# One decode step of attention and MLP: 512 rows of wo over eight DMA engines in place of 320 over five

## The chip, the cores and the metric

The kernel runs on one core of one Trainium2 chip. The metric is the device time of one execution, in microseconds (us); a kernel is timed several times, and its median is given. A profile is of one execution more: its span runs from the first instruction to the last, and its own time is some two microseconds longer than that span. Engines go by these names: PE does the matmuls (PEld its weight loads), DVE and ACT work on vectors, POOL on little here, and SP issues the DMAs. Sixteen DMA engines move the data of the core. A DMA is cut into packets, which are spread over some or all of the sixteen; it has landed when the last packet of its last engine has.

## The reference, cut to what matters

One token is computed, with 32 heads of 128 and the last 4096 keys and values of a cache of 32768 each. Beside attention stands a small MLP on the same normalized x, and its SiLU gates the attention's output:

```
W = min(4096, max(256, Sk // 4))                    # 4096
q = (x @ wq).reshape(B, Sq, Hq, Dh)                 # x: 1 x 512, wq: 512 x 4096
scores = einsum("bhqd,bhkd->bhqk", q, k[last W]) * (Dh ** -0.5)
p = softmax(scores)
o = einsum("bhqk,bhkd->bhqd", p, v[last W])
s = o.reshape(B, Sq, Hq * Dh) @ wo                  # wo: 4096 x 512
...
xn = layernorm(A_x)
return A_x + s * silu(B(xn, w1, w2, w3, w4))
```

All tensors are bf16. The keys and values that are read are 32 MB each, wq and wo 4 MB each, the MLP's weights that are read some 3.3 MB. Row r of wo belongs to head r // 128.

## The kernel before, in words

Heads are taken in groups of four (`G = 4`), so there are eight groups, 0 to 7. For each group one DMA of 4 MB loads the keys (K0 to K7) and one the values (V0 to V7), 32 KB for each of 128 partitions; K0 comes in two pieces and V7 in three (`cuts = (0, 64, 112, CP)`, line 509: 64, 48 and 16 of the 128 columns). The main loop (line 514) has steps s = 0 to 9. Step s computes the scores of group s, the softmax of group s - 1 and the products with the values of group s - 2 (`LAG = 2`). The scores are shared: DVE multiplies and sums some of the columns (`k_vector`, lines 304 to 311), and PE transposes the others, ACT copies them out, and PE multiplies them with q (`k_turn`, `k_scores`). `v_part` (line 417) multiplies probabilities with values, one small matmul a column, and `v_out` (line 440) scales the result to o.

All loads go out from SP, in the order of the program (`load`, line 78). The buffers set when: three for keys, two for values. V7's first load, for instance, has to wait until PE is done with V5.

The product with wo is taken in blocks of heads as they come ready (`blocks`, line 385): heads 0 to 15 in `y_wide`, heads 16 to 23 in `y_block(1)`, and the last eight heads, 24 to 31, in pieces, all summed in one PSUM tile `y_ps`:

- **The few** (`wo_few`): the first FEW = 8 * 8 * NE rows of head 24 on; with NE = 5 these are 320 rows, that is heads 24 and 25 and half of head 26. `load_few` (line 398) loads them with two DMAs. Each has 4 * NE partitions with 8 rows each, which lie together in memory, so that a packet is 8 KB; its outermost dimension in memory is NE, and it runs on NE engines. The tile has 64 partitions, 32 for each DMA; what the loads do not fill is zeroed by POOL (line 522). `ox_few` (line 478) brings o into the same order with a small matmul, whose selection tile `few` is built at lines 264 to 269, and `y_block(few_block)` multiplies in 8 x 4 matmuls.
- **The rows** (`wo_rows`): the rest, head by head, 1 KB for each partition. `load_rows` (line 408) loads them: first, ahead of V7, the second half of head 26 (64 rows, on partitions 64 to 127; the first half of that tile is zeroed by POOL, line 524) and head 27 (128 rows); then, behind V7's three pieces, heads 28 and 29 in one DMA and heads 30 and 31 in one each. `y_head` (line 505) multiplies one head in 4 matmuls.

Group 6 is heads 24 to 27, group 7 heads 28 to 31. The few and the rows of heads 26 and 27 thus need o of group 6 alone, the last four heads need o of group 7. The last step (lines 597 to 606) runs on PE in this order: V7's first 64 columns, the few, heads 26 and 27 (lines 600 and 601), V7's other two pieces, and after `v_out` heads 28 to 31. DVE then multiplies with the gate and adds x, and SP writes the output (lines 608 to 612). The order of PE, DVE and ACT in the loop is that of the program (`tc.manual_schedule`).

The queue of SP, with what concerns the change, is at its end: ... V5, wo of heads 16 to 23, the two loads of the few, V6, the two loads of heads 26 and 27, V7 in three pieces, heads 28 and 29, head 30, head 31, output.

Of the kernel before, what the change touches and what calls it, by code (L numbers as in the profile page):

```python
# [8 lines left out]
P = 128  # L9
# [9 lines left out]
G = 4  # L19
LAG = 2  # L20
K_BUFS = 3
NE = 5
V_BUFS = 2
EARLY = 2
LATE = 7
# [4 lines left out]
def kernel(  # L30
# [14 lines left out]
    nc = tc.nc  # L45
# [3 lines left out]
    _, H, Sk, Dh = A_k_cache.shape  # L49
# [28 lines left out]
    def load(dst, src):  # L78
        return tc.keep_in_program_order(nc.sync.dma_start(out=dst, in_=src))
# [17 lines left out]
    def load_kv(pool, cache, g, cuts=(0, CP)):  # L97
        t = pool.tile([P, CP, Dh], BF16, tag="kv", name="kv")
        src = cache[0, G * g:G * g + G, W0:, :].rearrange("a (b c) d -> b a (c d)", b=PB)
        dst = t[:].rearrange("p c d -> p (c d)")  # L100
        for c0, c1 in zip(cuts, cuts[1:]):
            load(dst[:, c0 * Dh:c1 * Dh], src[:, :, c0 * Dh:c1 * Dh])
        return t
# [43 lines left out]
    def rows_add(ps, col, w, last):  # L147
        k = col.shape[0]
        for j in range(KC):
            nc.tensor.matmul(ps[32 * j:32 * j + 1, :], lhsT=col, rhs=w[0:k, j * P:(j + 1) * P],  # L150
                             start=False, stop=last, skip_group_check=True)
# [114 lines left out]
    for c in range(2):  # L266
        nc.vector.tensor_copy(
            out=few[:, c, 0:4 * NE].rearrange("p (a b) -> p a b", b=4),
            in_=ident_bf[:, 4 * NE * c:4 * NE * (c + 1)].rearrange("p (b a) -> p a b", b=4))

# [27 lines left out]
    def k_open(g):  # L298
        st[g] = {
            "sT": ps_s.tile([P, CP - 64, G], FP32, tag="sT", name="sT"),  # L300
            "S": sm_pool.tile([P, CP], FP32, tag="S", name="S"),
        }

    def k_vector(g, kn, part):
        m = nd(g) // 4
        rows = slice(m * part, m * part + m)
        prod = prod_pool.tile([P, 20, Dh], BF16, tag="prod", name="prod")
        nc.vector.tensor_tensor(out=prod[:, 0:m, :], in0=kn[:, rows, :],  # L308
                                in1=q_bc[:, g:g + 1, :].to_broadcast([P, m, Dh]), op=ALU.mult)
        nc.vector.tensor_reduce(out=st[g]["S"][:, rows], in_=prod[:, 0:m, :], axis=AX.X, op=ALU.add)  # L310
# [3 lines left out]
    def batches(g):  # L314
        n, m = nd(g), CP - nd(g)
        k = -(-m // 8)
        edges = [n + m * i // k for i in range(k + 1)]
        return list(zip(edges, edges[1:]))

    def k_turn(g, kn, b):  # L320
        c0, c1 = batches(g)[b]
        pt = ps_tr.tile([P, 8, P], BF16, tag="pt", name="pt")
        for c in range(c0, c1):
            nc.tensor.transpose(pt[:, c - c0, :], kn[:, c, :], ident_bf[:])  # L324
        kts[b] = kt_pool.tile([P, 8, P], BF16, tag="kt", name="kt")
        nc.scalar.copy(out=kts[b][:, 0:c1 - c0, :], in_=pt[:, 0:c1 - c0, :])  # L326

    def k_scores(g, b):
        kt = kts.pop(b)
        c0, c1 = batches(g)[b]  # L330
        for c in range(c0, c1):
            nc.tensor.matmul(st[g]["sT"][:, c - nd(g), :], lhsT=kt[:, c - c0, :],  # L332
                             rhs=qT_bf[:, G * g:G * g + G], start=True, stop=True)
# [39 lines left out]
    def sm_den(g):  # L373
        s = st[g]
        s["den"] = ps_misc.tile([P, G], FP32, tag="misc", name="den_ps")
        nc.tensor.matmul(s["den"][:], lhsT=ones_f[:], rhs=s["sum"][:], start=True, stop=True)  # L376

    def sm_rden(g):
        s = st[g]
        s["rden"] = sm_pool.tile([P, G], FP32, tag="rden", name="rden")  # L380
        nc.vector.reciprocal(out=s["rden"][:], in_=s["den"][:])  # L381
# [5 lines left out]
    few_h = blocks[few_block][0]  # L387
    FEW = 8 * 8 * NE
    h_part = few_h + FEW // P

    r_part = FEW % P
    o_blk, wo_blk, ox_blk = {}, {}, {}

    def load_wo(i):
        h0, n = blocks[i]
        load(wo_blk[i], A_wo[h0 * P:(h0 + n) * P, :].rearrange("(p t) n -> p t n", p=P))

    def load_few():
        t = wo_blk[few_block]
        for c in range(2):  # L400
            r0 = few_h * P + c * FEW // 2
            load(t[32 * c:32 * c + 4 * NE],
                 A_wo[r0:r0 + FEW // 2, :].rearrange("(b a t) n -> a b (t n)", b=4, a=NE))

    def wo_row(h):
        return wo_rows[:, h - h_part, :]

    def load_rows(h, n):
        if h == h_part:
            load(wo_rows[r_part:P, 0, :], A_wo[h * P + r_part:(h + 1) * P, :])  # L410
            h, n = h + 1, n - 1
        load(wo_rows[:, h - h_part:h - h_part + n, :],
             A_wo[h * P:(h + n) * P, :].rearrange("(h p) n -> p h n", p=P))

# [86 lines left out]
    def y_block(i):  # L501
        for t in range(8):
            rows_add(y_ps, ox_blk[i][:, t:t + 1], wo_blk[i][:, t, :], False)

    def y_head(h):
        rows_add(y_ps, o_blk[few_block][:, h - few_h:h - few_h + 1], wo_row(h), h == H - 1)
# [7 lines left out]
    for s in range(NG + LAG):  # L514
        h = s - LAG
        last = h == NG - 1
        kn = load_kv(k_pool, A_k_cache, s, (0, 64, CP) if s == 0 else (0, CP)) if s < NG else None
        if s == LAG:
            wts_guard.__exit__(None, None, None)
            v_pool = ctx.enter_context(tc.tile_pool(name="v", bufs=V_BUFS))  # L520
            wo_blk[few_block] = v_pool.tile([64, 8, D], BF16, tag="wo_few", bufs=1, name="wo_few")
            nc.gpsimd.memset(wo_blk[few_block][:], 0.0)
            wo_rows = v_pool.tile([P, H - h_part, D], BF16, tag="wo_rows", bufs=1, name="wo_rows")
            nc.gpsimd.memset(wo_rows[0:r_part, 0, :], 0.0)
        if last:
            load_rows(h_part, 2)
            v = load_kv(v_pool, A_v_cache, h, cuts)
            for r, n in ((H - G, 2), (H - 2, 1), (H - 1, 1)):
                load_rows(r, n)
        elif h >= 0:  # L530
            v = load_kv(v_pool, A_v_cache, h)
        if h == 3:
            wo_24 = k_pool.tile([P, 32, D], BF16, tag="kv", name="wo_24")
            wo_blk[0], wo_blk[1] = wo_24[:, 0:16, :], wo_24[:, 16:24, :]
            load_wo(0)
        if h == 5:
            load_wo(1)
            load_few()

        if s < NG:  # L540
            nb = len(batches(s))

            def keys(b0, b1):
                for b in range(b0, b1):
                    k_turn(s, kn, b)
                    if b > 0:
                        k_scores(s, b - 1)

            k_open(s)
            k_vector(s, kn, 0)  # L550
            keys(0, 2)
            if s > 1:
                sm_den(s - 2)
                sm_rden(s - 2)
            if h - 1 in MOVED:
                v_add(h - 1)
                v_out(h - 1)
            keys(2, 4)
            k_vector(s, kn, 1)
            if s > 0:  # L560
                sm_turn(s - 1)
            if s == 6:
                ox_spread(0)
            keys(4, nb)
            k_scores(s, nb - 1)
            sm_own(s)
            if s > 0:
                sm_exp(s - 1)
            k_vector(s, kn, 2)
            if s == 6:  # L570
                ox_pick(0)
            k_vector(s, kn, 3)
            if h >= 0:
                v_part(h, v)
            sm_max(s)
            if s == 6:
                y_wide(0, 0, 16)
            if h >= 0 and h not in MOVED:
                v_out(h)
        elif s == NG:  # L580

            sm_den(NG - 2)
            sm_rden(NG - 2)
            sm_turn(NG - 1)
            ox_spread(1)
            sm_exp(NG - 1)
            ox_pick(1)
            y_block(1)
            rows_add(y_ps, one_f, y_row, False)
            v_part(h, v)  # L590
            v_out(h)
            ox_spread(few_block)
            sm_den(NG - 1)
            sm_rden(NG - 1)
            ox_pick(few_block)
            ox_few(few_block)
        else:
            v_part(h, v, 0, cuts[1])
            y_block(few_block)
            for r in range(h_part, H - G):  # L600
                y_head(r)
            for c0, c1 in zip(cuts[1:], cuts[2:]):
                v_part(h, v, c0, c1)
            v_out(h)
            for r in range(H - G, H):
                y_head(r)
# [36 lines left out]
```

## Time and profile before

| what | value |
|---|---|
| median of 4 runs | 195.07 us (194.64 to 196.91) |
| profiled execution, its own time | 195.71 us |
| its span | 193.9 us |
| mean granted TensorE clock | 0.682 |
| read from HBM | 78.84 MB, 407 GB/s over the span |
| load queue of SP (q1) | 4554 packets, 96.0% of 16 engines' span |
| wo_few loads | 2 of 160 KB, issued from 131.16 us on |
| wo_rows loads ahead of V7 | 64 KB and 128 KB, issued from 151.04 us on |
| V7's three pieces | 2048, 1536 and 512 KB, issued from 172.21 us on |

How to read it: times within the profile count from the span's start. The profiled execution took 195.71 us, 0.64 us above the median of the runs. A DMA's share is the mean over the 16 engines, so that a share of 13/16 can mean that three of them have nothing to do. A share can come out a little over 1, since packets on one engine overlap by some nanoseconds and count where they start. Packets of the DMA queues named "instruction" carry program text to the engines.

### The profile page before, as it was taken

To read this page: it belongs to the slowest core of one execution; us is meant where nothing else is said; L and a number is where in the kernel's file an instruction comes from. 1 tells how busy PE (TensorE), PEld (TensorE's weight loads), DVE (VectorE), ACT (ScalarE), POOL (GpSimd) and SP (SyncE) were. 2 spreads that over 40 slices of the span, in tenths; PEclk is the share of its full clock that TensorE was granted. 3 is DMA by queue.
4 is the path that set the end of the run, shared out by engine and by line. 5 is a ranking of instruction groups with operands and counts; after the bars stand their busy time and mean duration, and the time that the engine had idled before them with its cause. 6 is when DMAs were issued, how large, how long until landed. Compare 5 with 4: busy or idle time off the path is not lost.

```text
span 193.9 us, 4769 instructions
## 1 busy us (share of the span) xinstructions
PE 134.5 (69%) x2123; PEld 102.5 (53%) x2123; DVE 143.8 (74%) x162; ACT 87.2 (45%) x195; POOL 6.4 (3%) x14
## 2 busy tenths in 40 slices
PE   0559761978746579697998978730788878854892
PEld 0453451867535433386985347730768246743771
DVE  1550109998999999999999999990899999951201
ACT  2003001889896360467577155720485059813000
POOL 2110008000000000000000000000000000000000
PEclk9999965586955558965555896855555599655555
DMA  6999999999999999999999999999999999999980
GB/s 213 419 450 365 379 429 478 426 433 422 433 422 433 433 428 429 433 433 433 436 429 439 422 439 389 470 422 422 439 433 431 426 429 397 465 411 369 418 332 14
DMA packets 4725, 79.13 MB, mean 408 GB/s; under 512 B 666, under 2 KB 1466, under 8 KB 1722
## 3 DMA queue, kind: packets, MB, share of 16 engines
q1 hardware_dynamic: 4554, 78.84, 96.0%
q8 instruction: 16, 0.26, 0.5%
q10 hardware_dynamic: 152, 0.00, 0.0%
q14 instruction: 3, 0.02, 0.0%
HBM read 78.84 MB, written 0.00 MB: 407 GB/s over the span
## 4 chain that ended last, share of the span: by engine, by line
DMA 38%; DVE 33%; PE 16%; ACT 9%; issue 2%; SPq 0%; ACTq 0%
DMA kv<-in_A_k_cache_dram 29%; DVE S L310 19%; DVE prod L308 11%; DMA kv<-in_A_v_cache_dram 8%; ACT kt L326 7%; PE oT L430 5%; PE pt L324 4%; PE yr_ps L496 3%; PE sT L332 2%; DMA x_bf<-in_A_x_dram 2%; ACT o L453 1%; PE den_ps L376 1%; PE oT L437 1%; DVE S L346 1%; PE mb_ps L363 1%
## 5 line engine op out<-in xcount | busy, mean ns | idle before, releaser
L310 DVE TENSOR_REDUCE S<-prod 128x20 f32<-128x2560 bf16 (+2 forms) x32 | 82.2, 2570 | 1.1
L326 ACT COPY kt<-pt 128x1024 bf16<-128x1024 bf16 (+1 forms) x56 | 54.5, 1006 | 23.9 <-PE pt L324 23.2
L324 PE MATMUL pt<-ident_bf,kv 128*128 128x128 bf16 x444 | 46.7, 275 | 10.9 <-DMA kv<-in_A_k_cache_dram 10.9
L308 DVE TENSOR_TENSOR prod<-kv,q_bc 128x2560 bf16<-128x2560 bf16 (+2 forms) x32 | 43.5, 1359 | 8.5 <-DMA kv<-in_A_k_cache_dram 5.6
L324 PEld LDWEIGHTS <-kv 128*128 128x128 bf16 x444 | 37.7, 126 | 12.9 <-DMA kv<-in_A_k_cache_dram 11.2
L332 PE MATMUL sT<-qT_bf,kt 128*128 128x4 bf16 x444 | 20.7, 168 | 15.9 <-ACT kt L326 15.3
L332 PEld LDWEIGHTS <-kt 128*128 128x128 bf16 x444 | 17.1, 104 | 23.8 <-ACT kt L326 23.7
L430 PE MATMUL oT<-pT,kv 128*128 128x4 bf16 x768 | 22.0, 166 | 5.4 <-issue 3.6
L430 PEld LDWEIGHTS <-kv 128*128 128x128 bf16 x768 | 21.3, 104 | 7.4 <-issue 4.1
L422 PE MATMUL ov<-kv,pT 128*16 128x512 bf16 x64 | 17.5, 441 | 0.0
L370 ACT ACTIVATE pT<-S,mb 128x128 bf16<-128x128 f32 x32 | 13.9, 569 | 0.3
L422 PEld LDWEIGHTS <-pT 128*16 128x16 bf16 x64 | 6.3, 101 | 10.2 <-issue 4.6
L453 ACT ACTIVATE o<-oT,rden 128x1 bf16<-128x1 f32 x24 | 4.3, 261 | 11.8 <-PE oT L430 7.6
L449 DVE TENSOR_TENSOR o<-oT,rden 128x4 bf16<-128x4 f32 x2 | 0.3, 162 | 12.3 <-PE oT L430 12.3
L341 ACT ACTIVATE own<-sT,par 128x48 f32<-128x48 f32 (+2 forms) x32 | 7.6, 360 | 3.7 <-PE sT L332 3.7
L370 ACT ACTIVATION_READ_ACCUMULATOR pT<-S,mb 128x1 f32 x32 | 8.2, 255 | 0.0
L425 ACT COPY ov_sb<-ov 16x512 f32<-16x512 f32 x2 | 1.1, 575 | 13.2 <-PE ov L422 13.2
L231 DVE COPY hr<-hr_ps 1x512 f32<-1x512 f32 x1 | 0.7, 678 | 8.1 <-PE hr_ps L228 8.1
L496 PE MATMUL yr_ps<-wo,ox 128*1 128x512 bf16 x16 | 5.9, 545 | 0.9 <-DVE ox L474 0.9
L220 ACT ACTIVATE a_bf<-a_ps 128x10 bf16<-128x10 f32 x1 | 0.2, 180 | 11.8 <-PE a_ps L217 11.8
L363 PE MATMUL mb_ps<-md,par_t 5*128 5x4 f32 x16 | 4.2, 330 | 1.7 <-DVE md L358 1.0
L354 PE MATMUL mt_ps<-ident_f,m 128*1 128x128 f32 x8 | 2.8, 346 | 3.6 <-DVE rden L381 3.6
(117 smaller groups left out, 90.5 us busy)
## 6 DMA issues: line engine op xcount, KB each, us to landing
kv<-in_A_k_cache_dram SPq DMA_DIRECT2D x7, 4096.0 KB, 30.2
kv<-in_A_v_cache_dram SPq DMA_DIRECT2D x7, 4096.0 KB, 34.2
wq_sb<-in_A_wq_dram SPq DMA_DIRECT2D x1, 4096.0 KB, 19.5
kv<-in_A_k_cache_dram SPq DMA_DIRECT2D x2, 2048.0 KB, 24.9
wo<-in_A_wo_dram SPq DMA_DIRECT2D x1, 2048.0 KB
kv<-in_A_v_cache_dram SPq DMA_DIRECT2D x1, 2048.0 KB, 11.8
kv<-in_A_v_cache_dram SPq DMA_DIRECT2D x1, 1536.0 KB, 14.8
w_sb<-in_B_w_dram SPq DMA_DIRECT2D x1, 1376.0 KB
```

What stands on the lines that cost most here:

```text
L308: nc.vector.tensor_tensor(out=prod[:, 0:m, :], in0=kn[:, rows, :], in1=q_bc[:, g:g + 1, :].to_broadcast([P, m, Dh]), op=ALU.mult)
L310: nc.vector.tensor_reduce(out=st[g]["S"][:, rows], in_=prod[:, 0:m, :], axis=AX.X, op=ALU.add)
L324: nc.tensor.transpose(pt[:, c - c0, :], kn[:, c, :], ident_bf[:])
L326: nc.scalar.copy(out=kts[b][:, 0:c1 - c0, :], in_=pt[:, 0:c1 - c0, :])
L332: nc.tensor.matmul(st[g]["sT"][:, c - nd(g), :], lhsT=kt[:, c - c0, :], rhs=qT_bf[:, G * g:G * g + G], start=True, stop=True)
L341: nc.scalar.mul(s["own"][:, 0:m, a], s["sT"][:, 0:m, a], par[:, a:a + 1])
L363: nc.tensor.matmul(mb_ps[:], lhsT=par_t[:].rearrange("k b a -> k (b a)"), rhs=md[:], start=True, stop=True)
L370: nc.scalar.activation(out=s["pT"][:, :, a], in_=s["S"][:], func=ACT.Exp, scale=scale, bias=mb[:, a:a + 1], accum_out=s["sum"][:, a:a + 1])
L422: nc.tensor.matmul(s["ov"][:], lhsT=s["pT"][:, c:c + 4, :].rearrange("p i a -> p (i a)"), rhs=v[:, c:c + 4, :], start=(c == 0), stop=(c == ...
L430: nc.tensor.matmul(s["oT"][:], lhsT=v[:, c, :], rhs=s["pT"][:, c, :], start=(c == 0), stop=(c == CP - 1))
L453: nc.scalar.mul(o_blk[b][:, c + k:c + k + 1], st[g]["oT"][:, k:k + 1], st[g]["rden"][:, k:k + 1])
L496: nc.tensor.matmul(yr[i][:], lhsT=ox_blk[i][:, t:t + 1], rhs=wo_blk[i][:, t, :], start=(t == 0), stop=(t == n - 1))
```

## The change

NE goes from 5 to 8. The few then are 8 * 8 * 8 = 512 rows, which are heads 24 to 27 in full: two DMAs of 32 partitions each, 256 KB each, with an outermost dimension of 8. The 64 partitions of the tile are then all filled. No rows of heads 26 and 27 are left for `wo_rows`: its tile has four heads in place of six, the two loads ahead of V7 are gone, the memset for half a head too, and `y_head` runs for heads 28 to 31 alone. The bytes that are loaded are the same in all. The diff:

```
-NE = 5
+NE = 8
...
     FEW = 8 * 8 * NE
     h_part = few_h + FEW // P
-
-    r_part = FEW % P
+    assert FEW % P == 0 and h_part == H - G
...
     def load_rows(h, n):
-        if h == h_part:
-            load(wo_rows[r_part:P, 0, :], A_wo[h * P + r_part:(h + 1) * P, :])
-            h, n = h + 1, n - 1
         load(wo_rows[:, h - h_part:h - h_part + n, :],
              A_wo[h * P:(h + n) * P, :].rearrange("(h p) n -> p h n", p=P))
...
             wo_rows = v_pool.tile([P, H - h_part, D], BF16, tag="wo_rows", bufs=1, name="wo_rows")
-            nc.gpsimd.memset(wo_rows[0:r_part, 0, :], 0.0)
         if last:
-            load_rows(h_part, 2)
             v = load_kv(v_pool, A_v_cache, h, cuts)
...
             v_part(h, v, 0, cuts[1])
             y_block(few_block)
-            for r in range(h_part, H - G):
-                y_head(r)
             for c0, c1 in zip(cuts[1:], cuts[2:]):
```

More of the change, by code (lines that the diff above doesn't have):

```diff
@@ L21 @@
 K_BUFS = 3
-NE = 5
+NE = 8
 V_BUFS = 2
@@ L389 @@
     h_part = few_h + FEW // P
-    r_part = FEW % P
+    assert FEW % P == 0 and h_part == H - G
     o_blk, wo_blk, ox_blk = {}, {}, {}
@@ L408, in load_rows @@
     def load_rows(h, n):
-        if h == h_part:
-            load(wo_rows[r_part:P, 0, :], A_wo[h * P + r_part:(h + 1) * P, :])
-            h, n = h + 1, n - 1
         load(wo_rows[:, h - h_part:h - h_part + n, :],
@@ L523 @@
             wo_rows = v_pool.tile([P, H - h_part, D], BF16, tag="wo_rows", bufs=1, name="wo_rows")
-            nc.gpsimd.memset(wo_rows[0:r_part, 0, :], 0.0)
         if last:
-            load_rows(h_part, 2)
             v = load_kv(v_pool, A_v_cache, h, cuts)
@@ L599 @@
             y_block(few_block)
-            for r in range(h_part, H - G):
-                y_head(r)
             for c0, c1 in zip(cuts[1:], cuts[2:]):
```

## The prediction, made before the changed kernel ran

> **What bounds the kernel now.** I read the page first: the busy table, the DMA row of the slices, the table of queues, and the chain. No engine is full, but the 16 DMA engines are.
>
> ```profile
> span 193.9 us, 4769 instructions
> PE 134.5 (69%) x2123; PEld 102.5 (53%) x2123; DVE 143.8 (74%) x162; ACT 87.2 (45%) x195; POOL 6.4 (3%) x14
> DMA  6999999999999999999999999999999999999980
> ...
> q1 hardware_dynamic: 4554, 78.84, 96.0%
> q8 instruction: 16, 0.26, 0.5%
> ```
>
> The load queue (q1) keeps the engines 96.0% busy from start to end: what counts is how many bytes each engine has to move, and which engine ends last. A second traffic shares them: 16 fetches of program text, 16 KB each. Their 0.5% is 0.005 x 16 x 193.9 / 16 = 0.97 us for one.
>
> Then the chain of waits in its order of time, for the end alone:
>
> ```profile
> 172.82 14.83 DMA kv<-in_A_v_cache_dram
> 187.65 0.05 issue
> 187.70 1.88 PE oT L430 x64
> 189.58 0.02 issue
> 189.61 0.17 DVE o L449
> 189.78 0.04 issue
> 189.82 0.69 PE y_ps L150 x14
> ```
>
> The end hangs on the second piece of the last values (48 columns of V7), which lands at 187.65. After it come 64 small matmuls, the scaling of o, and the products with wo's last four rows of heads.
>
> Then the timeline of the same stretch, for PE's own work ahead of that landing:
>
> ```profile
> 184.08 1.87 PE L430 MATMUL oT<-pT,kv 128*128 128x4 bf16 x64
> ...
> 186.53 0.80 PE L150 MATMUL y_ps<-wo_few,of 64*1 64x128 bf16 x23 [0.19 <-issue]
> 187.26 0.10 PEld L150 LDWEIGHTS <-o 128*1 128x1 bf16 x8 [0.22 <-issue]
> 187.26 0.38 PE L150 MATMUL y_ps<-wo_rows,o 128*1 128x128 bf16 x8
> 187.70 1.79 PEld L430 LDWEIGHTS <-kv 128*128 128x128 bf16 x64 [0.33 <-DMA kv<-in_A_v_cache_dram]
> ```
>
> PE ends its products for heads 26 and 27 at 187.64, 0.01 us before the landing. So two things end there together, and a gain needs both.
>
> Last, the quarter-microsecond windows at the end (PE busy, clock, DMA share, GB/s):
>
> ```profile
> 185.75:186.00 0.25, 0.25 (x16) 0.50 1.11 451
> 186.00:186.25 0.25, 0.25 (x9) 0.50 0.82 336
> 186.25:186.50 0.25, 0.10 (x2) 0.50 0.81 336
> ...
> 188.50:188.75 0.25, 0.25 (x16) 0.50 0.65 225
> 189.00:189.25 0.25, 0.25 (x16) 0.50 0.53 184
> 189.50:189.75 0.25, 0.07 (x3) 0.50 0.10 33
> ```
>
> This is a staircase: the engines do not end together. From 186.0 the share is 0.81 to 0.82, which is 13 of 16: three engines have nothing left 3.5 us before the last one stops. The trace's packet records, which no view prints, say the same when a packet is put on the engine whose last packet ended where it begins: three engines end at 186.1, 186.1 and 186.5, the rest between 187.8 and 189.9.
>
> **Why they end apart.** In those records eight engines take the 16 KB fetches of q8 in turn, and each fetch delays its engine by about 1.5 us. The other eight take none. Five of these carry the two wo_few loads (their 8 KB packets show it), the last three are the early ones. A load on five engines uses the lowest five, so the engines without fetches hold 0 to 4; the set is most simply 0 to 7, and then the three idle engines are 5, 6 and 7, the ones that the change loads. This step is an inference: no row names an engine.
>
> **The change part by part.**
>
> 1. wo_few grows from 320 rows on five engines to 512 on eight. Engines 0 to 4 carry the same 64 KB as before (eight packets of 8 KB), engines 5 to 7 get 64 KB new. Rate: between 100 and 164 us q1 moved 27.40 MB at 99.6% of 16 engines, so 27.40 MB / (0.996 x 16 x 64 us) = 26.9 KB a microsecond per engine, and 65.5 KB take 2.44 us. The three idle engines would end at 188.6, 188.6 and 188.9 in place of 186.1 to 186.5: below the last, at no cost. Without that cover the price is 2.44 us at full length.
>
> 2. The 64-row and the 128-row load (wo_rows for heads 26 and 27, in the queue between V6 and V7) go: 4 + 8 packets of 1 KB on every engine. From 188.5 to 190.3 only such packets run: 30.7% of 16 engines for 1.8 us, 187 rows and 27 completions, so 8.84 / 187 = 0.047 us a row, 0.57 us for twelve; their starts in the records are 0.042 apart, which gives 0.52. I take 0.52. All of V7 and the last four heads' rows move up by it: the 187.65 landing to 187.13, the landing of the last row of heads (190.17 in the trace's landings; its four matmuls begin at 190.21) to 189.65.
>
> 3. On PE the 8 matmuls of heads 26 and 27 go: 0.38 us, on the path between the few products and the landing. PE then comes free at 187.26 at the latest; and as the first V7 piece lands 0.52 earlier than its 184.03, PE's 64 matmuls can begin at about 183.9 in place of 184.08, held then by the spread of o. So PE is free at 187.05 to 187.26, against a landing at 187.13: the 64 matmuls begin at 187.18 to 187.31, 0.39 to 0.52 earlier.
>
> 4. From there to the last row's products it is 189.82 - 187.70 = 2.12, and 0.28 more for heads 28 to 30: 189.58 to 189.71, beside a row that lands at 189.65. The end moves from 190.21 to about 189.70, by **0.5 us**. The output's part behind it stays.
>
> 5. SP issues two DMAs less (151.04 to 152.38, in a stretch where it waits until 172.21 anyway) and two wo_few loads of 32 partitions each in place of 20, at 131.16: beside SP's wait until 150.41, nothing. V7's first load is issued at 172.21, because its buffer comes free then; today's earliest engine asks for it at 174.55, behind the two row loads. Without them, but with the new 64 KB, the earliest asks at about 175.5: cover of over 2 us. The small memset on POOL (0.52 us at 32.5) was waited for by no one. The 512 rows need the same 32 matmuls as the 320, and one copy of each spread tile.
>
> 6. One unknown: between 174.0 and 179.5 the load queue moves 378 GB/s at a share of 0.99, against 430 elsewhere. That is 5.5 x (1 - 378/430) = 0.67 us lost, of which the small rows' own overhead is some 0.1. It coincides with the two row loads, but the rows at the end slow no neighbour (the 12 KB and 4 KB packets beside them keep 0.46 and 0.16 us). If the removed rows caused it, 0.55 us more are won; if not, nothing. The nearest row is that end stretch, so I take nothing and keep 0.55 for the range.
>
> **Sum.** Against the profiled execution (195.71 us, span 193.9, 1.8 around it): 195.2. It stands 0.64 above the median of the runs, 195.07, so the forecast for the median is 195.07 - 0.5 = **194.6**.
>
> **A rule against the change.** Three engines end early by the windows above. The Trainium skill, "DMA: Bandwidth & Descriptors", "Rules for kernel authors", says to use all 16 engines, as a short outermost dimension confines a DMA to few. Taken alone it would price the step as 2.4 us on three engines against 0.5 off all: 1.9 us slower where all end together. The staircase says they do not.
>
> **The rivals.**
>
> *The new 64 KB fall on an engine that is already late* (one mechanism, the other sign). For: the engine numbers are inferred. Against: eight fetch-free engines, five of them the lowest. An engine gains 2.44 and loses 0.52, so 1.92 net; it decides from engines whose last row lands after 190.17 - 1.92 = 188.25, and in the landings twelve of the sixteen do. Earliest of these 188.8: end 190.7, 0.5 later, 195.6. Latest without wo_few 189.9: 191.8, 1.65 later, 196.7.
>
> *PE takes over* (the transfer is hidden). If V6 lands no earlier (178.69, its slowest engine keeps its load) and PE's chain from there is nearly without gaps, only its removed 0.38 us, or less where the instruction stall ahead of 186.53 grows, come through: 0 to 0.3, so 194.8 to 195.1. For: the 0.01 us between both. Against: the 0.33 us that PE's weight loads stood idle for the landing.
>
> *The dip of step 6 goes as well*: 0.9 to 1.1 in all, 194.0 to 194.2.
>
> **How the numbers follow.** Forecast (0.3 to 0.8 us won, 194.3 to 194.8): 0.58. Late engine: 0.16. PE: 0.16. Dip gone: 0.10. The range runs from the dip's 194.0, with 0.1 for the scatter of the median (the runs shown spread from 194.64 to 196.91), to 195.8 on the late engine's side, which leaves out most of its upper half: 193.9 to 195.8; the forecast's own is 194.2 to 194.9. One per cent is 1.95 us, about what a measurement of this kernel can tell from no change. The cases lie between -1.1 and +1.65, so only scatter on top reaches either bound: faster 0.03, within 0.92, slower 0.05.
>
> **What the profile would show.** Steps 1 and 2: the staircase starts later, with the share near 1 until about 187, and the last bytes move at about 189.3; page totals keep 78.84 MB, with 192 packets of 1 KB fewer and 24 of 8 KB more. Step 2: V7's second landing near 187.1. Step 3: the few products followed at once by V7's 64 matmuls. Step 4: y at about 190.0 in place of 190.54. Step 6: GB/s from 174 to 179. The prediction is wrong if the share falls to 13 of 16 early again while the last bytes move later (the wrong engines were loaded), or if PE waits no more for V7's second piece and yet ends no earlier.

## The result, and the profile after

The changed kernel takes 195.54 us (median of 54 runs), the kernel before 195.13 (78 runs): a ratio of 1.0025, interval 1.0012 to 1.0038. It is slower by 0.4 to 0.5 us where 0.5 us less was forecast. The profiled execution of the changed kernel took 196.96 us, 1.4 above its median; a second one, below, took 195.49 and shows the same end. The difference between the two lies at the start: wq lands 19.7 us after its issue in the first and 18.3 in the second. The kernel before has both starts too (19.5 us in its first profile, 18.3 in its second). So first profiles are compared with first ones and second with second ones, and landings are counted from the first landing of wo's second block (heads 16 to 23), the last load ahead of the few.

First the page of the changed kernel, in the lines shown of before:

```profile
span 195.1 us, 4750 instructions
PE 133.8 (69%) x2115; PEld 101.6 (52%) x2115; DVE 143.9 (74%) x162; ACT 87.0 (45%) x195; POOL 6.0 (3%) x13
DMA  6999999999999999999999999999999999999960
...
q1 hardware_dynamic: 4360, 78.84, 95.4%
q8 instruction: 16, 0.26, 0.5%
```

The change did what it says: the bytes are the same, the packets 194 fewer, PE has 8 matmuls less, and the fetches of program text are still 16. Its chain of waits at the end:

```profile
173.40 15.49 DMA kv<-in_A_v_cache_dram
188.88 0.05 issue
188.93 1.88 PE oT L426 x64
190.81 0.02 issue
190.84 0.17 DVE o L445
191.01 0.04 issue
191.05 0.71 PE y_ps L150 x16
```

The same end hangs on the same landing, V7's second piece, which comes at 188.88 in place of 187.65; counted from wo's second block it is 23.77 us in place of 22.90. Behind it nothing has changed: 2.12 us to the last rows' products, as before. Ahead of it, PE's timeline:

```profile
180.45 3.58 PE L426 MATMUL oT<-pT,kv 128*128 128x4 bf16 x128 [2.79 <-DMA kv<-in_A_v_cache_dram]
...
185.65 1.86 PE L426 MATMUL oT<-pT,kv 128*128 128x4 bf16 x64
187.45 1.02 PE L150 MATMUL y_ps<-wo_few,of 64*1 64x128 bf16 x32
188.93 1.87 PE L426 MATMUL oT<-pT,kv 128*128 128x4 bf16 x64 [0.46 <-DMA kv<-in_A_v_cache_dram]
```

V6 lands late too: PE begins its 128 matmuls at 180.45 in place of 178.73. It is now clearly the transfers that PE waits for, in both places. And the windows at the end (PE busy, clock, DMA share, GB/s) tell which transfers:

```profile
188.75:189.25 0.50, 0.32 (x12) 0.50 0.29 109
189.25:189.75 0.50, 0.50 (x25) 0.50 0.10 39
189.75:190.25 0.50, 0.50 (x25) 0.50 0.14 49
190.25:190.75 0.50, 0.50 (x21) 0.50 0.14 47
190.75:191.25 0.50, 0.25 (x14) 0.50 0.08 29
```

A share of 0.10 to 0.14 is two engines of sixteen (0.125). From 189.3 to 191.1 two engines work alone, while fourteen have nothing left. The other end of the staircase is still there too: two engines, where it was three, have their last row at 186.75 and 186.80, and the next ones at 187.6 and 188.2. This is in substance the sign that the prediction named for the wrong engines having been loaded: some engines run dry early again, and the last bytes move later.

### The profile page after: what moved, and what is told of

Same layout as the page of the kernel before. It is cut to its first block, busy times and chain, and to the rows that moved or that the text cites. A ratio compares the mean times of both kernels' runs of the same rounds, so it can differ in the third digit from the quotient of the medians.

```text
span 195.1 us, 4750 instructions
## 1 busy us (share of the span) xinstructions
PE 133.8 (69%) x2115; PEld 101.6 (52%) x2115; DVE 143.9 (74%) x162; ACT 87.0 (45%) x195; POOL 6.0 (3%) x13
## 3 DMA queue, kind: packets, MB, share of 16 engines
q1 hardware_dynamic: 4360, 78.84, 95.4%
## 4 chain that ended last, share of the span: by engine, by line
DMA 39%; DVE 32%; PE 16%; ACT 8%; issue 3%; SPq 0%; ACTq 0%
DMA kv<-in_A_k_cache_dram 29%; DVE S L310 19%; DVE prod L308 10%; DMA kv<-in_A_v_cache_dram 8%; ACT kt L326 7%; PE oT L426 5%; PE pt L324 5%; PE yr_ps L492 3%; PE sT L332 2%; DMA x_bf<-in_A_x_dram 2%; PE den_ps L376 1%; PE oT L433 1%; DVE S L346 1%; ACT own L341 1%; DVE m L348 0%
## 5 line engine op out<-in xcount | busy, mean ns | idle before, releaser
L324 PE MATMUL pt<-ident_bf,kv 128*128 128x128 bf16 x444 | 45.6, 270 | 11.6 <-DMA kv<-in_A_k_cache_dram 11.6
L324 PEld LDWEIGHTS <-kv 128*128 128x128 bf16 x444 | 36.9, 124 | 13.7 <-DMA kv<-in_A_k_cache_dram 12.0
L426 PEld LDWEIGHTS <-kv 128*128 128x128 bf16 x768 | 21.2, 103 | 10.1 <-issue 5.3
L418 PE MATMUL ov<-kv,pT 128*16 128x512 bf16 x64 | 18.7, 464 | 0.0
## 6 DMA issues: line engine op xcount, KB each, us to landing
wq_sb<-in_A_wq_dram SPq DMA_DIRECT2D x1, 4096.0 KB, 19.7
```

What stands on the lines that cost most here:

```text
L418: nc.tensor.matmul(s["ov"][:], lhsT=s["pT"][:, c:c + 4, :].rearrange("p i a -> p (i a)"), rhs=v[:, c:c + 4, :], start=(c == 0), stop=(c == ...
L426: nc.tensor.matmul(s["oT"][:], lhsT=v[:, c, :], rhs=s["pT"][:, c, :], start=(c == 0), stop=(c == CP - 1))
```

## The experiments

Theory A: two of the engines 5 to 7 also take fetches of program text, were late already, and the new 64 KB make them the last. Against it stood that PE's own chain had grown (B), that the first profile was of an unusual execution (C), that any load over eight engines costs (D), and that the two engines are late for another reason than fetches (E). No row of a trace names an engine; the numbers are the prediction's, by which a load on n engines uses 0 to n - 1, so that engine 5 is the one that a load on six engines adds. The ratio given is always to the kernel before on the same chip.

**1. Both kernels once more, for a second profile of each.** No edit.

> The changed kernel once more, for a second profiled execution. Theory A (two of the engines 5 to 7 also take fetches of program text, so the new 64 KB each make them the last): again two engines run alone at the end, V6 lands at about 180.4 and V7's second piece at about 188.9 where those two had two fetches before, earlier where they had fewer; the executions fall in two groups near 195.4 and 196.7. Theory B (the engines are idle as predicted, and the loss is PE's): V6 lands near 178.7 as before and PE's chain is what is longer. Theory C (the loss in that profile was of one execution, and the usual one ends evenly): no engine alone at the end, ratio 1.00.

> The kernel before once more, for a second profiled execution; ratio 1.000. All theories: three engines run dry more than 3 us before the last one, if the first profile was a usual execution; if the fetches begin on another engine in this one, the landings differ by steps of about 1.5 us, and V7's second piece lands between 186.5 and 188.5.

Measured: changed 1.0024 (1.0001 to 1.0047), before 0.9985 (0.9964 to 1.0005). Both second profiles have the quick start (wq lands after 18.3 us), and among them the changed kernel takes 195.49 against 194.95: 0.54 more. Its V7's second piece lands at 187.46 against 186.57 (23.85 and 22.89 us after wo's second block), its last row at 190.0 against 189.1. Two engines are alone again at the end, three run dry early again in the kernel before. C falls, and so does B: V6 lands at 179.0 against 177.6. PE's last steps ahead of V7's second piece, in the second profile of before and then of the changed kernel:

```profile
185.89 0.80 PE L150 MATMUL y_ps<-wo_few,of 64*1 64x128 bf16 x23 [0.64 <-issue]
186.93 1.86 PE L430 MATMUL oT<-pT,kv 128*128 128x4 bf16 x64
```

```profile
187.50 1.87 PE L426 MATMUL oT<-pT,kv 128*128 128x4 bf16 x64 [0.40 <-DMA kv<-in_A_v_cache_dram]
```

**2. Six and seven engines.** `NE = 6` leaves head 27 as 1 KB rows, `NE = 7` half of it. For six engines, against the changed kernel:

```
-NE = 8
+NE = 6
...
         if last:
+            load_rows(h_part, 1)
...
             y_block(few_block)
+            for r in range(h_part, H - G):
+                y_head(r)
```

And for seven engines, against the kernel before:

```
-NE = 5
+NE = 7
...
-            h, n = h + 1, n - 1
+            return
...
-            load_rows(h_part, 2)
+            load_rows(h_part, 1)
```

> 384 rows over the lowest six engines, head 27 left as 1 KB rows. Theory A: if engine 5 takes fetches, one engine runs alone at the end and the time is 195.4; if it is the idle one, none does, and the time is that of before less 0.2 us (the 64-row load that is gone): 194.9. Theory B: 194.9. Theory C: 194.9.

> 448 rows over the lowest seven engines, 64 rows of head 27 left as 1 KB rows. Theory A: if engine 7 is one of the two that take fetches, only one engine runs alone at the end; if 5 and 6 are the two, both do, and the time is that of the changed kernel, 195.5. Theory B: 194.7, as the few and the rows are the same work as before. Theory C: 194.8.

Measured: six engines 1.0062 (1.0038 to 1.0087), seven 1.0078 (1.0048 to 1.0107, four runs): 196.08 and 196.55 us, where 195.4 and 195.5 were expected. The pattern of late engines came as theory A has it for 5 and 6, the times did not. These are the times at which V7's second piece lands on each of the 16 engines, from the trace's landings (first profiles for NE = 5 and 8; the one with seven engines had the quick start, the others not, so only the pattern within a row counts):

```
NE = 5  184.0 184.0 184.3 | 185.6 186.3 186.3 186.4 186.9 187.0 187.1 187.1 187.1 187.2 187.3 187.4 187.7
NE = 6  183.5 183.5 183.7 | 184.9 185.8 185.8 185.8 186.6 186.6 186.7 186.7 186.8 186.8 186.9 187.1 | 188.9
NE = 7  182.9 183.1 183.2 | 184.5 184.6 184.9 184.9 185.0 185.8 185.8 185.9 185.9 185.9 186.2 | 188.1 188.1
NE = 8  184.2 184.2 | 185.0 185.1 185.7 185.8 185.8 185.8 186.5 186.6 186.7 186.7 186.8 187.0 | 188.8 188.9
```

With the sixth engine one lands alone, with the seventh two, and the three early ones are all still there; with the eighth no further one is late, and one of the three early ones is gone. So the sixth and the seventh engine, 5 and 6, were not among the idle ones, and of the three idle ones only one was in reach, engine 7. The windows say so as well; with six engines and with seven:

```profile
189.75:190.25 0.50, 0.50 (x25) 0.50 0.06 23
190.25:190.75 0.50, 0.50 (x21) 0.50 0.07 25
```

```profile
189.00:189.50 0.50, 0.50 (x25) 0.50 0.14 49
189.50:190.00 0.50, 0.50 (x19) 0.50 0.13 45
```

0.06 is one engine, 0.13 are two. Both kernels are slower than the changed one as it ran beside them, though they load fewer engines: six engines by 0.6 us (its interval overlaps that of the changed kernel a little), seven by 1.1. At the landing of V7's second piece, counted from wo's second block, the differences are smaller: 24.04 us with six engines and 24.32 with seven, against 23.77 and 23.85. The 128-row load that six engines keep is worth 0.34 us by step 2's price, the 64-row load that seven keep 0.17, and some 0.35 more for the packets that it slows (see the prediction's step 6, below): that is enough for the landings. The rest of the times, some 0.3 us and 0.6, stays open.

**3. The two halves of the change by themselves.** First the kernel before without its two row loads, so that these 192 rows of wo are left out of the result, then the changed kernel with them put back for no one to read.

```
         if last:
-            load_rows(h_part, 2)
```

> The kernel before without its two loads of heads 26 and 27 ahead of V7 (these rows of wo are left out and zero); the products with them stay. It prices the removal alone. Theory A (the removal gives what step 2 said and the five to eight engines' load takes it back): every engine is 0.52 us earlier behind V6, ratio 0.9975, about 194.6; less, where PE ends as late as the landing. Theory B (the removal gives nothing, as PE is the path): ratio 1.000.

Measured: 0.9964 (0.9943 to 0.9986), 0.70 us less (0.27 to 1.11). The removal is worth what step 2 said, and more at the landing: V7's second piece lands 21.94 us after wo's second block, in place of 22.89, which is 0.95 earlier where step 2 had 0.52.

```
         if last:
+            load(wo_rows[64:P, G, :], A_wo[26 * P + 64:27 * P, :])
+            load(wo_rows[:, G + 1:G + 2, :], A_wo[27 * P:28 * P, :]...)
```

> The changed kernel with two loads of 64 and 128 rows of 1 KB put back ahead of V7, whose data no one reads. It prices the eight-engine load alone. Theory A: the two engines that run alone at the end do so 0.5 us later still, 0.5 us over the changed kernel: ratio to before 1.005, about 196.0; V7's second piece lands some 24.4 us after the first landing of wo's second block, against 22.9 in the kernel before and 23.85 in the changed one. Theory B (PE): the same as the changed kernel, 195.5.

Measured: 1.0066 (1.0053 to 1.0079), 1.29 us more than before. V7's second piece lands 24.60 us after wo's second block first does (188.31 against 163.71), 1.70 later than in the kernel before. The eight-engine load alone costs 1.29, the removal alone gives 0.70; together that is 0.59 slower, against 0.5 measured for the change. The halves add up within their intervals.

**4. Half the load over eight engines.** 256 rows, 32 KB an engine; 16 rows of 1 KB an engine ahead of V7.

```
-    FEW = 8 * 8 * NE
+    FEW = 4 * 8 * NE
...
-        for c in range(2):
+        for c in range(1):
...
```

> 256 rows over eight engines (32 KB each in place of 64), heads 26 and 27 as 1 KB rows ahead of V7. Theory A: engines 5 and 6 end 1.2 us earlier than in the changed kernel less 0.7 us for the 16 rows an engine that are back: 0.5 us earlier, ratio to before 1.000 (0.998 to 1.003), V7's second piece 23.3 us after the first landing of wo's second block. Theory D (any load on eight engines in place of five costs, however small): as slow as the changed kernel, 1.0025 or more.

Measured: 1.0001 (0.9983 to 1.0019). V7's second piece lands 23.2 us after wo's second block (186.8 against 163.6), 23.3 was expected. Two engines still have their last row 1.0 us after the others (189.3 against 188.3). That a load runs over eight engines costs nothing that can be told here (the interval leaves 0.37 us); D falls.

**5. The changed kernel with half the program text on PE.** All loads stay; what it computes is no longer attention.

```
-        for c in range(c0, c1):
+        cs = list(range(c0, c1)) if g >= 6 else list(range(8))
...
-        for c in range(c0, c1):
+        for c in range(c0, c0 + 2):
             nc.tensor.transpose(pt[:, c - c0, :], kn[:, c, :], ident_bf[:])
...
-        for c in range(KC):
+        for c in range(1):
             nc.tensor.matmul(qT_ps[:, h:h + 1], ...)
```

> The changed kernel with about half of PE's instructions left out (most products with values of groups 1, 3, 4, 5, six of eight transposes of a batch, three quarters of q's products; the results are not attention's). All loads stay. It tells whether the fetches of program text are what makes engines 5 and 6 late. Theory A: 8 to 10 fetches of 16 KB in place of 16, and the two engines, with one fetch each in place of two, end 1.5 us earlier against the first landing of wo's second block: V7's second piece lands 22.3 to 22.9 us after it in place of 23.85, and the stretch at the end in which two engines run alone is under 0.5 us in place of 1.8. Theory E (engines 5 and 6 are late for another reason, by their place or their share of the loads): it stays at 23.8 and the two still run alone for 1.5 us or more.

Measured: 0.9946 (0.9928 to 0.9964), with two runs. Its queues, and the windows of its end:

```profile
q1 hardware_dynamic: 4360, 78.84, 96.1%
q8 instruction: 9, 0.15, 0.3%
```

```profile
186.50:187.00 0.50, 0.50 (x25) 0.50 0.39 127
187.00:187.50 0.50, 0.50 (x24) 0.50 0.26 90
187.50:188.00 0.50, 0.38 (x15) 0.50 0.21 74
188.00:188.50 0.50, 0.37 (x12) 0.50 0.03 10
```

Nine fetches in place of 16, the same 4360 packets of data, and the stretch with two engines alone is gone: three engines now have their last row within 0.14 us of each other (188.36 to 188.50), the fourth 0.6 us earlier. V7's second piece lands 22.35 us after wo's second block (185.97 against 163.62), in place of 23.85, 1.5 us earlier. E falls: it is the fetches that make engines 5 and 6 late. Two other ways in which less text could help are answered by the landings. The transfers as a whole are no faster: V6 lands on its first engine 9.72 us after wo's second block, 9.67 in the changed kernel's second profile, and only its last engine is earlier, 13.86 in place of 15.43. And V7's loads do go out 7.6 us earlier (163.58 in place of 171.16), but the last engine is busy with V6 long after either issue (until 177.5 here, 179.0 there), and from V6's last landing to that of V7's first piece it is 4.83 us here and 4.77 there. That PE did less is not what the end gained from: it waited for the same landing, with 0.33 us idle ahead of it.

**6. Less program text with the result kept.** In the kernel before, the values of more groups are multiplied in 32 wide matmuls in place of 128 small ones.

```
-MOVED = (0, 2)
+MOVED = (0, 2, 4)
```

> The kernel before, with the values of group 4 multiplied as in groups 0 and 2: 32 wide matmuls in place of 128 small ones, 192 PE instructions fewer. The result is the same. It asks whether less program text alone is a gain in a whole kernel. Theory A (a fetch costs its engine 1.5 us): 15 fetches in place of 16; if the engine that is spared one is not among the last, nothing, if it is, up to 0.5 us: ratio 0.997 to 1.000. Theory F (PE's 10 us more in that step delay the keys' step and the release of buffers): 1.002 or more, with loads that start late.

> The same for groups 1, 3 and 4: 576 PE instructions fewer, 13 or 14 fetches in place of 16. Theory A: three engines are spared 1.5 us each; the last landing is then that of the engines that carry wo_few, 0.2 to 0.7 us earlier: ratio 0.996 to 0.999. Theory F: PE, with 30 us more work, holds back the loop: ratio 1.01 or more, DMA share under 0.95 in the middle of the span.

Measured: 1.0066 (1.0032 to 1.01) and 1.0216 (1.0167 to 1.0265): theory F, by which PE's longer work holds back the buffers. A could not show in them: the first kernel still has 16 fetches, where 15 were expected, and the second, with 14, is held back by PE. PE's longer step holds V5's buffer, V7's loads go out at 174.72 in place of 172.21 (in the second kernel at 176.31), and engines that are done with V6 from 174.6 on have to wait. SP's timeline of the first:

```profile
156.13 1.23 SPq L79 DMA_DIRECT2D wo_rows<-in_A_wo_dram  x2
174.72 1.86 SPq L79 DMA_DIRECT2D kv<-in_A_v_cache_dram  x3
```

**7. The load fitted to what engines 5 and 6 had to spare.** The first load of the few over eight engines, the second over five: 416 rows, and 96 rows of 1 KB.

```
-NE = 5
+NES = (8, 5)
...
-    FEW = 8 * 8 * NE
+    FEW = 4 * 8 * sum(NES)
```

> The first load of the few over eight engines, the second over five: engines 0 to 4 carry 64 KB as before, 5 to 7 carry 32 KB, and 96 rows of head 27 stay as 1 KB rows, 6 an engine in place of 12. Theory A: engines 5 and 6 get 1.22 us and lose 0.26, just what they had to spare (they were 1.0 us ahead of the last in the kernel before, as 1.92 us net made them 0.95 later than it); all others gain 0.26. Ratio to before 0.9985 to 1.000, about 195.0: it should equal the kernel before or beat it by a hair, and beat the changed kernel by 0.5 us. Theory D (any load on eight engines costs): 1.002 or more.

Measured: 0.9992 (0.9965 to 1.0019), 195.16 against 195.42. It cannot be told from the kernel before. That it would beat the changed kernel by 0.5 us, as expected, was not measured side by side; the two ratios differ by 0.0033. No kernel tried that computes all of the result beats it clearly.

## Why the prediction was wrong

**The step that failed** is the inference ahead of the parts: "the set is most simply 0 to 7, and then the three idle engines are 5, 6 and 7". What was read from the trace held: eight engines take the fetches, eight do not, five of these carry the few, and three end early. That the eight are a row of neighbours stood in no line. By experiment 2 the engines without fetches are 0 to 4, 7, and two from 8 to 15; 5 and 6 take fetches. So the price "2.44 us at full length" without cover, named in step 1, fell due on two of the three engines, less what these two had to spare: with the row loads in place (experiment 3) the landing that the end hangs on came 1.70 us later, and the time rose by 1.29.

**The rival that came true** is the late engine, at a chance of 0.16: 0.5 to 1.65 us later was its span. The landing of V7's second piece moved by 0.9 us, counted from wo's second block (0.87 in the first profiles, 0.96 in the second), the time by 0.4 to 0.5, at the lower end of that span. The time moved less than these landings, as executions of the kernel before differ in what ends last: in its second profile PE itself stood still 0.64 us ahead of the few's last 23 products, and V7's piece was there (186.57) before PE was (186.93). What PE stood still for, the profile does not show; program text is likely, as it is the same place in the program as in the first profile.

**Step by step.** Step 1's size fits: of 2.44 us, 1.70 came through at the landing, so engines 5 and 6 were some 0.7 us ahead of the last one. Half the load costs no time that can be told, as experiments 4 and 7 show. Step 2 was mis-sized: 0.52 was taken, and the landing moved by 0.95 (the time by 0.70, 0.27 to 1.11). Step 3 was right for PE's own work, and mattered little: PE waits for the landing now (0.46 us by its matmuls). Step 4's 2.12 us came out the same; the row that the end waits for in the last place lands behind it again. Step 5 was right in that nothing of SP's or POOL's shows; its 175.5 for the earliest engine was not (it begins V7 at 174.67), as two of the three early engines got no load. Step 6 took nothing for the dip, and that is where the rest of step 2's price lies. The window of the changed kernel that answers to 174.0 to 179.5 of before:

```profile
174.40:179.90 5.50, 2.31 (x43) 0.50 0.95 402
```

402 GB/s in place of 378. In the same stretch of the other profiles it is 392 and 393 with both row loads (experiment 3, and the second profile of before) and 380 with the 64-row load alone (seven engines), but 403 with the 128-row load alone (six engines), 402 with 256 rows in one load (experiment 4), and 407 and 410 without any (changed, second profile; experiment 3). So it is the 64-row load, which fills half of the 128 partitions, that goes with the dip. The packet records say how: between 172 and 180 us the 16 KB and 32 KB packets, which take 0.61 and 1.21 us undisturbed, take 6.7 and 5.2 us longer in sum in the two profiles of before, 4.2 with the rows put back, 6.5 with seven engines and 7.8 in experiment 7, which has a load of 96 rows. In the two of the changed kernel, with six engines and in experiments 3 (without rows) and 4 it is 0.5 to 1.3. The difference between before and changed is 4 to 5.5 us over 16 engines, 0.25 to 0.35 us for each, which went with the load. The rows at the end, from which the prediction took its nothing, are loads of all 128 partitions. Why a load of part of them slows the packets beside it was not tried.

**The rule that spoke against the change**, that a short outermost dimension confines a DMA to few engines, was weighed against the staircase and set aside. The staircase showed that some engines had room, not that those which the DMA would reach did. By the rule alone the change was to be 1.9 us slower where all end together, 2.4 of it the load: 0.4 to 0.5 was measured for the change, and 1.29 for the eight-engine load alone.

The Trainium skill, "Runtime: NRT & Kernel Launch", "Instruction fetch mechanics", says that an engine fetches its text in blocks of 16 KiB, 256 instructions, through a DMA queue of its own, and calls the cost of a crossing mostly hidden. The count agrees: 2 x 2115 PE instructions are 16.5 blocks, and 16 fetches are seen; 2 x 1207 are 9.4, and 9 are seen. The cost is not hidden here, as the DMA engines are the bound: with 9 fetches in place of 16 the landing that the end hangs on came 1.5 us earlier, which is what one fetch takes of an engine.

## What to carry to other kernels

Where DMA engines are the bound, the one that ends last counts, and room on some engines is worth something only if the next load reaches those. Which engines a load on few of them takes was not free here: each step of NE added one to the same others. So add one engine at a time and look how many land alone, before the bytes are moved. Count the program text as traffic: with some 43% of PE's instructions left out (1207 matmuls in place of 2115) the changed kernel, which was 0.25% slower than the one before, was 0.54% faster than it, though it waited for the same bytes. And look at the packets beside a small load, not only at its own.

## What the runs showed of the hardware

- The fetches of PE's program text do not spread over all 16 engines: in the packet records of the two first profiles they go round eight. The engines that a load of the few adds as its sixth and seventh are among them, its first five and its eighth are not. A fetch takes about 1 us of its engine for 16 KB (0.94 to 1.11 in these two profiles), where a data packet of 16 KB takes 0.61, and the packet behind it is 0.46 to 0.55 longer: about 1.5 us in all.
- A load of 64 or 96 rows of 1 KB, which fills part of the partitions, went with longer packets beside it (4.2 to 7.8 us in sum over 16 engines, in five profiles); loads of 128 or 256 rows did not (0.5 us, in two). The cause is open.
- The 4 MB load of wq lands 18.3 us after its issue in some executions and 19.5 to 19.7 in others, of both kernels, and the whole stream behind it moves by as much. What makes the difference was not tried.
- The loads of the few land on 5, 6, 7 and 8 engines, as their outermost dimension says, and each step up added one engine to the same others, as far as the landings tell them apart.
